# Casts of q and k placed behind a mask, and the end of the first group reordered, in a fused sliding-window attention and MLP kernel

## The chip, the cores and the metric

The kernel runs on one core of one Trainium2 chip. The metric is the device time of one execution in microseconds (us), as a median over runs. Five engines work side by side and each takes its instructions in order: TensorE (PE: matrix products and transposes), VectorE (DVE), ScalarE (ACT), GpSimd (POOL) and SyncE (SP, which here issues nearly all DMAs). An instruction that waits for another engine holds up everything behind it on its own engine.

## The reference, cut to what matters

Eight batches of attention with eight heads of 64 columns over 576 rows, each row seeing itself and the 63 rows before it; then, on the 512 columns of all heads together, a row normalisation, two matrix products with a ReLU between them, and the attention output added.

```python
scores = scale * np.matmul(q, k.transpose(0, 1, 3, 2))          # scale = 1/8
mask = (rel >= 0) & (rel < 64)                                  # rel = row - column
attn = np.exp(np.where(mask, scores, -1e9) - max)               # divided by its row sum
x = np.matmul(attn, v)                                          # heads side by side: (8, 576, 512)
xn = (x - mean(x)) / np.sqrt(var(x) + 1e-6) * g_ln
out = x + np.maximum(xn @ w_ch1, 0.0) @ w_ch2                   # 512 -> 2048 -> 512
```

Inputs and output are float32; the products run in float16 with float32 sums.

## The kernel before, in words

**Groups.** The first 512 rows of each batch are a group (0 to 7); the last 64 rows of all batches are gathered into group 8, called the tails, whose steps are numbered by pairs of batches. While the MLP of group g runs on PE, the attention of batch b = g + 1 is worked into it, and q, k and v of batch g + 2 are loaded, cast and transposed. The MLP is a list of units (`mlp_units`): for group 0 half units and row units (`l1_half`, `l1_rows`), then full units (`l1`), then the second product (`l2_three`, `l2`); for group 1 sixteen half units (first the columns of rows 0 to 255, `half` 0, then `half` 1), then `l2`; from group 2 on sixteen `l1` units and fourteen `stage` units, which make the second product in seven smaller ones from sums (`s_sums`, `w2_sums`, both on DVE).

**The order is written out by hand.** `at(i, f, ...)` puts an attention step into slot i, and slot i is issued after unit i. Within a slot the order of the `at` calls counts, engine by engine. So a step's place in the list decides both when PE comes to it and what stands behind it on every engine that it uses.

**One attention step** (a block of 128 rows, j or kb = 0 to 3) consists of
- `s_pe` (L308): 32 small score products on PE into two PSUM banks; `home` says which: `sc` (pool `ps_s`), `xps` (pool `ps_x`, two banks in one tile) or `t` (the two transpose banks t0 and t1);
- `s_exp` (L344): two exponentials on ACT into `pt`, one for each parity of the heads;
- `s_mask` (L353): one DVE product of `pt` (128x1024) with the 0/1 mask, both operands in SBUF;
- `b_pe` (L366): 16 value products on PE, again into `xps`, `sc` or `t`;
- `b_rows` (L388): on DVE the reciprocal of the row sums, the division, mean and variance; for batches 0 and 1 also z (L428), which for steps (1, 0) and (1, 1) is made on ACT (L433) in `z_step`;
- `z_step` (L421): from batch 2 on, four POOL instructions (L437 to L443);
- `zt_step` (L452): z transposed into zT, the operand of the MLP's first product. For batches 0 and 1 PE transposes into a t bank and ACT copies it out (L465); later ones are DMA transposes issued by SP.

**q and k.** `load_qk` (L84) issues the loads on SP in two halves, `cast_qk` (L141) casts each to float16 on POOL (L147, 128x1024), and `t_main` (L261) transposes: eight PE transposes into a t bank and one copy out, by ACT for q (x = 0) and DVE for k (x = 1) unless `eng` says otherwise. From batch 3 on q goes through SP's DMA transpose instead, and k is copied out by ACT. The t banks t0 and t1 alternate; from a certain unit of a group on, only t0 is used (`tbank["shared"]`), because t1 then holds a result of the second product. `add_out` (L523, L526) reads that result on DVE.

**Around the change.** At the end of group 0 slots 22 to 30 hold batch 1's value steps 0 and 1, the z rows that follow, the transposes of the second half of q and k, and the scores and exponentials of steps 2 and 3. Group 1's slot 0 holds the four casts for batch 2; its slots 2 to 7 hold value steps 2 and 3, their z rows and batch 2's transposes. In groups 2 to 5 slot 5 holds three casts for batch g + 2 (the fourth is in slot 11), and the last mask before the value steps of slot 7: step 3 of batch b in groups 2 and 4, a step of the tails in groups 3 and 5 (`TAILS`).

Of the kernel before, what the change touches and what calls it, by code (L numbers as in the profile page):

```python
# [11 lines left out]
FP16 = mybir.dt.float16  # L12
# [8 lines left out]
def kernel(  # L21
# [42 lines left out]
    mbias = p_const.tile([128, 64], FP16, tag="mbias", name="mbias")  # L64
    magt = p_const.tile([128, 4], FP32, tag="magt", name="magt")
    gT = p_const.tile([128, NKC], FP32, tag="gT", name="gT")
    mhalf = p_const.tile([128, 1], FP32, tag="mhalf", name="mhalf")
    w1g = p_const.tile([128, NKC, HID], FP16, tag="w1g", name="w1g")
    w2s = p_const.tile([128, NHC, DM], FP16, tag="w2s", name="w2s")
# [4 lines left out]
    def t_tile(shape, name):  # L74
        i = 0 if tbank["shared"] else tbank["n"] % 2
        tbank["n"] = i + 1
        return ps_t.tile(shape, FP16, tag=f"t{i}", name=name)
# [183 lines left out]
    def t_main(b, x, half, eng=None):  # L261
        src = qk16.pop((b, x, half))
        if b >= XQ and x == 0:
            dst = flat(b)[:, 2 * SM * half:2 * SM * half + 2 * SM]
            nc.sync.dma_start_transpose(out=dst.rearrange("p (a t) -> p a t", t=128),
                                        in_=src[:, :].rearrange("p a e d -> p (a e d)"))
            return
        j = 2 if b < 2 else 4
        tp = t_tile([128, 8, 128], f"tp_{b}_{x}_{half}")
        for i in range(8):  # L270
            nc.tensor.transpose(out=tp[:, i, :], in_=src[:, i], identity=ident16)  # L271
        if b < 2:
            c0 = 64 * x + 256 * half
            dst = qkT[b][x][:, :, c0:c0 + 256]
        else:
            dst = qkT[b][x][:, 2 * half:2 * half + 2, 64 * x:64 * x + 512]
        evac(x if eng is None else eng, dst.rearrange("c h (p j) -> c h p j", j=j),
             tp[:, :].rearrange("c (h j) p -> c h p j", j=j))

    def t_tail(i, x):  # L280
        src = tail16[i][x]
# [62 lines left out]
    def s_exp(g, j, *pars):  # L344
        pt, sc = pts[(g, j)], scs[(g, j)]
        for par in pars:
            o, i = pt[:, par], sc[par][:, :, :, :]
            if XQ <= g < NGRP - 1:
                o = o.rearrange("p h w (r j) -> p (h w) r j", j=4)
                i = i.rearrange("p h w (j r) -> p (h w) r j", j=4)  # L350
            nc.scalar.activation(out=o, in_=i, func=AF.Exp, bias=0.0, scale=scale)  # L351

    def s_mask(g, j):  # L353
        pt = pts[(g, j)]
# [622 lines left out]
    for g in range(NGRP):  # L977
# [7 lines left out]
        def at(i, f, *a):  # L985
            slots[min(i, len(slots) - 1)].append((f, a))
# [10 lines left out]
        if g == 0:  # L997
            at(1, zt_step, 0, 2, "dve")
            at(2, zt_step, 0, 3, "dve")
            at(4, newton, 0, 0, 4)  # L1000
            at(11, t_main, 1, 0, 0, 1)
            at(12, t_main, 1, 1, 0, 1)
            at(16, s_pe, 1, 0)
            at(16, s_pe, 1, 1, False, "xps")
            at(16, s_exp, 1, 0, 0, 1)
            at(16, s_mask, 1, 0)
            at(17, s_exp, 1, 1, 0, 1)
            at(17, s_mask, 1, 1)
            for c in range(2):
                at(20, vB_cur, 1, c, 0)  # L1010
                at(20, vB_prev, 1, c, 0)
            at(22, b_pe, 1, 0)
            at(22, b_pe, 1, 1, "sc")
            at(22, b_rows, 1, 0)
            at(22, z_step, 1, 0)
            at(23, b_rows, 1, 1)
            at(23, minus_mean, 1, 1)
            at(24, zt_step, 1, 0)
            at(25, z_step, 1, 1)
            at(26, t_main, 1, 0, 1, 0)  # L1020
            at(26, zt_step, 1, 1)
            at(27, t_main, 1, 1, 1, 1)
            at(27, vB_cur, 1, 2, 0)
            at(28, vB_prev, 1, 2, 0)
            at(28, vB_cur, 1, 3, 0)
            at(29, s_pe, 1, 2)
            at(29, s_pe, 1, 3, False, "t")
            at(29, s_exp, 1, 2, 0, 1)
            at(29, s_mask, 1, 2)
            at(30, s_exp, 1, 3, 0, 1)  # L1030
            at(30, s_mask, 1, 3)
        if g == 1:
            at(0, cast_qk, 2, 0)
            at(0, cast_qk, 2, 1)
            at(2, b_pe, 1, 2)
            at(2, b_pe, 1, 3, "sc")
            at(2, b_rows, 1, 2)
            at(3, b_rows, 1, 3)
            at(4, zt_step, 1, 2)
            at(4, root, 1)  # L1040
            at(6, zt_step, 1, 3)
            at(4, alloc_v, 2)
            at(4, alloc_qkT, 2)
            for c in (0, 2):
                at(5, cast_v, 2, c, c + 2)
                at(5, part_vB, 2, c)
            at(4, t_main, 2, 0, 0)
            at(5, t_main, 2, 1, 0)
            at(7, t_main, 2, 0, 1)
            at(7, t_main, 2, 1, 1)  # L1050
            at(7, w2_sums, 3, 0, 4)
            at(8, w2_sums, 3, 4, 8)
            at(25, w2_sums, 2, 0, 4)
            at(28, w2_sums, 2, 4, 8)
            at(9, s_pe, 2, 0)
            at(9, s_pe, 2, 1, False, "xps")
            at(9, s_exp, 2, 0, 0, 1)
            at(10, s_mask, 2, 0)
            at(11, s_exp, 2, 1, 0)
            at(12, s_exp, 2, 1, 1)  # L1060
            at(13, s_mask, 2, 1)
            for j in range(4):
                i = (14, 17, 20, 22)[j]
                if j < 3:
                    at(i, b_pe, 2, j)
                if j < 2:
                    at(i, s_mm, 2, j + 2)
                    at(i + 1, s_mask, 2, j + 2)
                if j == 2:
                    at(i, b_pe, 2, 3, "sc")  # L1070
                at(i, b_rows, 2, j)
                at(i, z_step, 2, j)
                at((18, 21, 24, 26)[j], z_act, 2, j)
                at((18, 21, 24, 26)[j], zt_step, 2, j)
            at(3, load_qk, 3, 0)
            at(8, load_qk, 3, 1)
            at(10, load_v, 3, 0, 4)
            at(8, alloc_qkT, 3)
            at(8, cast_qk, 3, 0)
            at(14, cast_qk, 3, 1, (0,))  # L1080
            at(17, cast_qk, 3, 1, (1,))
            at(22, alloc_v, 3)
            at(22, cast_v, 3, 0, 2)
            at(22, cast_v, 3, 2, 4)
            at(27, part_vB, 3, 0, 4)
            first_scores(3, 30)
            for i, (x, half) in zip((12, 24, 18, 28), ((0, 0), (1, 0), (0, 1), (1, 1))):
                at(i, t_main, 3, x, half, 0)
            at(40, load_qk, 4, 0)
            at(40, load_qk, 4, 1)  # L1090
            at(40, load_v, 4, 0, 2)
        if g == 2:
            for m, i in enumerate((1, 4)):
                at(4 + 2 * m, w2_sums, i, 0, 4)
                at(5 + 2 * m, w2_sums, i, 4, 8)
        if g > 1 and g + 2 < B:
            at(5, alloc_qkT, g + 2)
            at(5, cast_qk, g + 2, 0)
            at(5, cast_qk, g + 2, 1, (0,))
            at(11, cast_qk, g + 2, 1, (1,))  # L1100
        if g > 1 and b < B:
            tail = TAILS.get(g)
            at(2, b_pe, b, 0)
            at(2, b_rows, b, 0)
            at(2, z_step, b, 0)
            at(2, s_pe, b, 2)
            at(2, s_exp, b, 2, 0, 1)
            at(3, s_mask, b, 2)
            if tail:
                r, i = NGRP - 1, tail[0]  # L1110
                at(2, s_pe, r, i, False, "t")
                at(4, s_exp, r, i, 0)
                at(5, s_exp, r, i, 1)
                at(5, s_mask, r, i)
                at(7, b_pe, b, 1)
                at(7, b_pe, r, i, "t")
                at(7, s_mm, b, 3)
                at(7, b_rows, b, 1)
                at(7, z_step, b, 1)
                at(8, s_mask, b, 3)  # L1120
                at(8, b_rows, r, i)
                at(9, z_step, r, i)
                at(12, b_pe, b, 2)
                at(12, b_pe, b, 3, "sc")
                at(16, zt_step, r, i)
            else:
                at(2, s_pe, b, 3, False, "t")
                at(4, s_exp, b, 3, 0)
                at(5, s_exp, b, 3, 1)
                at(5, s_mask, b, 3)  # L1130
                at(7, b_pe, b, 1)
                at(7, b_pe, b, 2, "t")
                at(7, b_pe, b, 3, "sc")
                at(7, b_rows, b, 1)
                at(7, z_step, b, 1)
            at(12, b_rows, b, 2)
            at(12, z_step, b, 2)
            at(19, b_rows, b, 3)
            at(19, z_step, b, 3)
            for j in range(4):  # L1140
                at((2, 14, 18, {3: 25, 5: 25}.get(b, 23))[j], zt_step, b, j)
# [83 lines left out]
```

## Time and profile before

| what | value |
|---|---|
| median of 3 runs | 306.69 us (306.48 to 306.84) |
| the profiled execution | 306.86 us, its span 305.1 us |
| TensorE clock granted in it | 0.995 |
| casts of q and k (L147) on POOL | 30, 34.3 us busy, mean 1151 ns |
| masks (L358) on DVE | 32, 26.4 us busy, mean 831 ns |
| copies out of transposes (L257) on ACT | 17, 16.3 us busy, mean 961 ns |
| DMA queue q1 | 57.47 MB, 77.1% of 16 engines' span |

The span runs from the first to the last recorded instruction; the rest of an execution's time lies around it. A row of the timeline has the start in us from the beginning of the span, the duration in us, engine, line, operation, output and inputs with their shapes, and the number of instructions. A bracket at its end is the time that the engine stood idle just before the row, and what ended the wait. Products on PE are pipelined: the next one can start before the end that is shown for the one in front. Group 0's units begin near 21 us, group 1's near 56, group 2's near 92, and each later group takes some 31 us.

### The profile page before, as it was taken

The page shows a single profiled execution, that of the slowest core. Times are in us where ns is not written, and L with a number is a line of the kernel's source. Part 1 is how long each engine was busy: PE and PEld are TensorE (multiplying, and loading weights), DVE is VectorE, ACT ScalarE, POOL GpSimd, SP SyncE. Part 2 cuts the span into 40 slices and gives each one's busy share as a digit, 9 for nine tenths or more (in the row PEclk, how much of TensorE's full clock was granted, in tenths as well). Part 3 has the DMA queues.
Part 4 walks back from the last instruction along what each step waited for, and adds up shares of the span by engine and source line. Part 5 has one row for each costly group of instructions (what it writes and reads, how often), then busy time and mean ns, then how long its engine had stood idle before and what let it go on. Part 6 is the DMA issues. An engine that isn't in the chain of part 4 may idle for free.

```text
span 305.1 us, 7615 instructions
## 1 busy us (share of the span) xinstructions
PE 292.3 (96%) x3084; PEld 195.4 (64%) x3084; DVE 216.6 (71%) x420; ACT 155.2 (51%) x261; POOL 158.4 (52%) x230
## 2 busy tenths in 40 slices
PE   8999998999999999999999999999999999999992
PEld 3657544688454478546864686459745854788881
DVE  2879437675846896579667865697568775789972
ACT  4555655689348633874176528752575056306400
POOL 4689775451641896179509860886038407114300
PEclk9999999999999999999999999999999999999997
DMA  8999999999787898999189997992619395003014
GB/s 187 262 371 338 389 276 299 225 302 242 144 206 221 212 202 149 281 273 175 35 266 296 190 159 211 323 172 52 216 38 181 70 199 172 19 17 140 2 37 103
DMA packets 114533, 58.35 MB, mean 191 GB/s; under 512 B 83649, under 2 KB 105729, under 8 KB 114498
## 3 DMA queue, kind: packets, MB, share of 16 engines
q1 hardware_dynamic: 114208, 57.47, 77.1%
q8 instruction: 24, 0.39, 0.6%
q10 hardware_dynamic: 290, 0.40, 0.5%
q14 instruction: 11, 0.09, 0.1%
HBM read 38.80 MB, written 9.44 MB: 158 GB/s over the span
## 4 chain that ended last, share of the span: by engine, by line
PE 84%; DVE 4%; SPq 3%; ACT 3%; DMA 2%; POOL 1%; issue 1%; POOLq 0%
PE hps L504 28%; PE pA L581 12%; PE pB L581 8%; PE pC L581 8%; PE ch L516 5%; PE hph L646 5%; PE sc L341 3%; PE xps L385 3%; PE ch L681 3%; PE tp L271 2%; PE lA L719 2%; DMA w1s<-in_moe_w_ch_dram 2%; SPq L169 2%; ACT pt L351 2%; DVE pt L358 1%; SPq L89 1%
## 5 line engine op out<-in xcount | busy, mean ns | idle before, releaser
L504 PE MATMUL hps<-zT,w1g 128*128 128x512 f16 x416 | 94.7, 379 | 0.0
L508 ACT ACTIVATE hrT<-hps 128x512 f16<-128x512 f32 x104 | 62.4, 600 | 41.6 <-PE hps L504 38.3
L504 PEld LDWEIGHTS <-w1g 128*128 128x128 f16 x416 | 39.2, 98 | 45.4 <-issue 2.2
L351 ACT ACTIVATE pt<-sc 128x512 f16<-128x512 f32 x72 | 39.3, 600 | 23.2 <-PE sc L341 22.5
L437 POOL TENSOR_SCALAR rsz<-mvg 128x1 f32<-128x1 f32 x28 | 10.9, 390 | 75.1 <-DVE mvg L410 67.6
L581 PEld LDWEIGHTS <-sS 128*128 128x128 f16 x448 | 43.3, 98 | 4.9
L358 DVE TENSOR_TENSOR pt<-pt,mask 128x1024 f16<-128x1024 f16 x32 | 26.4, 831 | 21.0 <-ACT pt L351 21.0
L147 POOL CAST qk<-qk 128x1024 f16<-128x1024 f32 x30 | 34.3, 1151 | 9.2 <-DMA qk<-in_k_dram 3.3
L581 PEld LDWEIGHTS <-hrT 128*128 128x128 f16 x336 | 32.1, 98 | 6.4 <-ACT hrT L508 1.0
L257 ACT COPY qkT<-tp 128x1024 f16<-128x1024 f16 (+1 forms) x17 | 16.3, 961 | 23.8 <-PE tp L271 22.8
L581 PE MATMUL pC<-w2s,sS 128*128 128x256 f16 x224 | 26.9, 273 | 0.0
L581 PE MATMUL pA<-wT,sS 128*128 128x256 f16 x224 | 26.9, 273 | 0.0
L405 DVE TENSOR_TENSOR xn<-xps,rcp 128x256 f32<-128x256 f32 (+1 forms) x49 | 25.7, 547 | 0.8
L407 DVE BATCH_NORM_STATS2 stats<-xn 128x6 f32<-128x512 f32 x36 | 25.0, 695 | 1.2
L555 DVE TENSOR_TENSOR sS<-hrT 128x512 f16<-128x512 f16 (+1 forms) x40 | 23.7, 593 | 2.9 <-ACT hrT L508 2.9
L646 PE MATMUL hph<-zT,w1g 128*128 128x256 f16 x176 | 21.5, 273 | 0.9 <-ACT hrT L651 0.6
L401 DVE RECIPROCAL rcp<-xps 128x4 f32<-128x4 f32 (+1 forms) x49 | 7.8, 181 | 18.6 <-PE xps L385 18.6
L438 POOL TENSOR_TENSOR rsz<-rsz,mhalf 128x1 f32<-128x1 f32 x28 | 19.7, 702 | 2.3
L443 POOL TENSOR_SCALAR z<-xn,rsz 128x512 f16<-128x512 f32 x24 | 18.4, 767 | 2.5
L385 PEld LDWEIGHTS <-pt 128*64 128x64 f16 x576 | 11.6, 110 | 11.9 <-issue 5.8
L516 PE MATMUL ch<-w2s,hrT 128*128 128x512 f16 x80 | 18.8, 379 | 0.0
L646 PEld LDWEIGHTS <-w1g 128*128 128x128 f16 x176 | 16.4, 98 | 3.6 <-issue 1.1
(129 smaller groups left out, 438.2 us busy)
## 6 DMA issues: line engine op xcount, KB each, us to landing
out_dram<-xn SPq DMA_DIRECT2D x33, 256.0 KB, 3.3
qk<-in_q_dram SPq DMA_DIRECT2D x16, 512.0 KB, 6.1
qk<-in_k_dram SPq DMA_DIRECT2D x16, 512.0 KB, 6.8
v<-in_v_dram SPq DMA_DIRECT2D x28, 256.0 KB, 6.2
w2s<-in_moe_w_ch_dram SPq DMA_DIRECT2D x9, 512.0 KB, 7.8
w1s<-in_moe_w_ch_dram SPq DMA_DIRECT2D x4, 512.0 KB, 7.5
tk<-in_k_dram SPq DMA_DIRECT2D x8, 256.0 KB, 4.6
tv<-in_v_dram SPq DMA_DIRECT2D x8, 256.0 KB, 5.2
```

What stands on the lines that cost most here:

```text
L147: nc.gpsimd.tensor_copy(out=dst[:, :].rearrange("p (a j) e d -> p a e j d", j=j), in_=t[:, :].rearrange("p (a e j d) -> p a e j d", e=2, j ...
L351: nc.scalar.activation(out=o, in_=i, func=AF.Exp, bias=0.0, scale=scale)
L358: nc.vector.tensor_tensor(out=ptv, in0=ptv, in1=mb, op=ALU.mult)
L385: nc.tensor.matmul(out=tiles[h // n][64 * r:64 * r + 64, h % n, :D + 1], lhsT=pt[:, par, hp, r, :], rhs=rhs, start=True, stop=True)
L405: nc.vector.tensor_tensor(out=xn[:, n * i:n * i + n], in0=xps[:, :, 0:D], in1=rcp_b, op=ALU.mult)
L407: nc.vector.bn_stats(out=stats, in_=xv)
L504: nc.tensor.matmul(out=hps, lhsT=w1g[:, kc, 128 * hc:128 * (hc + 1)], rhs=zT[g][:, kc, :], start=(kc == 0), stop=(kc == NKC - 1),)
L508: nc.scalar.activation(out=hrT[:, hc, :], in_=hps, func=AF.Relu, bias=0.0, scale=1.0)
L516: nc.tensor.matmul(out=ch[kb], lhsT=hrT[:, hc, 128 * kb:128 * (kb + 1)], rhs=w2s[:, hc, :], start=(hc == 0), stop=(hc == NHC - 1),)
L555: nc.vector.tensor_tensor(out=o, in0=x, in1=y, op=op)
L581: nc.tensor.matmul(out=o, lhsT=a[:, c, 128 * p:128 * p + 128], rhs=wv[:, c, :], start=(first and (p == 0 or split_c) and c == 0), stop=(c ...
L646: nc.tensor.matmul(out=hps[:, e], lhsT=w1g[:, kc, 128 * hc:128 * (hc + 1)], rhs=zT[g][:, kc, 256 * half:256 * half + 256], start=(kc == 0) ...
```

## The change

The diff has two parts. In the first, a helper `after_mask` copies one element per partition of a masked `pt` tile on POOL into a new tile `masked` that nobody reads; POOL cannot run it before the mask is done. It is put ahead of the casts in slot 5 of groups 2 to 5, where it names the last mask of that slot (the calls move to a later place in the source, but stay in slots 5 and 11), and in group 1's slot 0 ahead of the last of the four casts, where it names the mask of batch 1's step 3.

In the second, for batch 1's second half, q and k are transposed into one tile in the `xps` pool (q in one bank, k in the other) instead of the t banks, and steps near them change slots. Group 0: q's transposes from slot 26 to 24, step 0's row transposes from 24 to 25, z of step 1 from 25 to 26, k's transposes from 27 to 26, step 1's row transposes from 26 to 27. The exponentials and the mask of step 3 go from the end of group 0 to slot 0 of group 1, so on ACT they stand behind the first unit's ReLU and not in front of it. Group 1: row transposes of steps 2 and 3 from slots 4 and 6 to 5 and 7, batch 2's second q transposes from 7 to 6. On PE, in the order of instructions, batch 2's q transposes now come before the rows' transposes of the same pair, and the k transposes after them.

No instruction is taken away; the five copies are all that is added.

```diff
+    masked = p_const.tile([128, 1], FP16, tag="masked", name="masked")
...
-        tp = t_tile([128, 8, 128], f"tp_{b}_{x}_{half}")
+        if (b, half) == (1, 1):
+            if x == 0:
+                both_tp[b] = ps_x.tile([128, 2, 8, 128], FP16, tag="xps", name=f"tp_{b}_{half}")
+            tp = both_tp[b][:, x]
+        else:
+            tp = t_tile([128, 8, 128], f"tp_{b}_{x}_{half}")
...
+    def after_mask(g, j):
+        nc.gpsimd.tensor_copy(out=masked, in_=pts[(g, j)][:, 1, NHP - 1, 1, 0:1])
...
-            at(24, zt_step, 1, 0)
-            at(25, z_step, 1, 1)
-            at(26, t_main, 1, 0, 1, 0)
-            at(26, zt_step, 1, 1)
-            at(27, t_main, 1, 1, 1, 1)
+            at(24, t_main, 1, 0, 1, 0)
+            at(25, zt_step, 1, 0)
+            at(26, z_step, 1, 1)
+            at(26, t_main, 1, 1, 1, 1)
+            at(27, zt_step, 1, 1)
...
-            at(30, s_exp, 1, 3, 0, 1)
-            at(30, s_mask, 1, 3)
         if g == 1:
+            at(0, s_exp, 1, 3, 0, 1)
+            at(0, s_mask, 1, 3)
             at(0, cast_qk, 2, 0)
-            at(0, cast_qk, 2, 1)
+            at(0, cast_qk, 2, 1, (0,))
+            at(0, after_mask, 1, 3)
+            at(0, cast_qk, 2, 1, (1,))
...
-            at(4, zt_step, 1, 2)
+            at(5, zt_step, 1, 2)
...
-            at(6, zt_step, 1, 3)
+            at(7, zt_step, 1, 3)
...
-            at(7, t_main, 2, 0, 1)
+            at(6, t_main, 2, 0, 1)
...
-        if g > 1 and g + 2 < B:
-            at(5, alloc_qkT, g + 2)
-            at(5, cast_qk, g + 2, 0)
-            at(5, cast_qk, g + 2, 1, (0,))
-            at(11, cast_qk, g + 2, 1, (1,))
...
+            if g + 2 < B:
+                at(5, alloc_qkT, g + 2)
+                at(5, after_mask, *((NGRP - 1, tail[0]) if tail else (b, 3)))
+                at(5, cast_qk, g + 2, 0)
+                at(5, cast_qk, g + 2, 1, (0,))
+                at(11, cast_qk, g + 2, 1, (1,))
```

More of the change, by code (lines that the diff above doesn't have):

```diff
@@ L277, in t_main @@
         evac(x if eng is None else eng, dst.rearrange("c h (p j) -> c h p j", j=j),
-             tp[:, :].rearrange("c (h j) p -> c h p j", j=j))
+             (tp if (b, half) == (1, 1) else tp[:, :]).rearrange("c (h j) p -> c h p j", j=j))
+    both_tp = {}
     def t_tail(i, x):
```

## The prediction

> **What bounds the kernel now.** I read the page's share table first, then TensorE's (PE's) own rows with the idle time in front of each, then VectorE (DVE) and GpSimd (POOL) at the same times.
>
> ```profile
> PE 292.3 (96%) x3084; PEld 195.4 (64%) x3084; DVE 216.6 (71%) x420; ACT 155.2 (51%) x261; POOL 158.4 (52%) x230
> ...
> PE 84%; DVE 4%; SPq 3%; ACT 3%; DMA 2%; POOL 1%; issue 1%; POOLq 0%
> ```
>
> PE is the bound. A reordering pays only where PE stands still, and the bracketed idle notes say where that is. The seven rows below hold 3.95 us of it at the places that the change touches.
>
> ```profile
> 48.44 0.40 PE L462 MATMUL ztp<-ident,z 128*128 128x128 f16 x4 [0.40 <-ACT z L433]
> ...
> 51.67 0.38 PE L462 MATMUL ztp<-ident,z 128*128 128x128 f16 x4 [1.09 <-DVE xn L526]
> ...
> 58.07 1.03 PE L646 MATMUL hph<-zT,w1g 128*128 128x256 f16 x8 [0.55 <-ACT hrT L651]
> ...
> 61.98 0.40 PE L462 MATMUL ztp<-ident,z 128*128 128x128 f16 x4 [0.39 <-DVE z L428]
> ...
> 132.59 0.45 PE L385 MATMUL xps<-vt,pt 128*64 128x65 f16 x16 [0.68 <-DVE pt L358]
> ...
> 164.04 0.22 PE L385 MATMUL xps<-vB,pt 128*64 128x65 f16 x1 [0.27 <-DVE pt L358]
> ...
> 195.34 0.45 PE L385 MATMUL xps<-vt,pt 128*64 128x65 f16 x16 [0.57 <-DVE pt L358]
> ```
>
> The last three are PE waiting for a mask (L358). Beside each mask stands a POOL cast of q or k:
>
> ```profile
> 130.95 1.04 POOL L147 CAST qk<-qk 128x1024 f16<-128x1024 f32 x1
> 130.97 1.56 DVE L358 TENSOR_TENSOR pt<-pt,mask 128x1024 f16<-128x1024 f16 x1 [1.97 <-ACT pt L351]
> ...
> 162.40 3.47 POOL L147 CAST qk<-qk 128x1024 f16<-128x1024 f32 x3
> 162.58 1.40 DVE L358 TENSOR_TENSOR pt<-pt,mask 128x1024 f16<-128x1024 f16 x1 [2.05 <-ACT pt L351]
> ...
> 193.70 3.61 POOL L147 CAST qk<-qk 128x1024 f16<-128x1024 f32 x3
> 193.84 1.45 DVE L358 TENSOR_TENSOR pt<-pt,mask 128x1024 f16<-128x1024 f16 x1 [2.01 <-ACT pt L351]
> ...
> 225.33 0.69 DVE L358 TENSOR_TENSOR pt<-pt,mask 128x1024 f16<-128x1024 f16 x1 [2.04 <-ACT pt L351]
> ```
>
> The fourth mask, in group 6, where no cast is queued, takes 0.69. The other three end 0.54, 0.54 and 0.55 us after the first cast's end (start + 1.04): the mask waits for the cast, whole, and then runs.
>
> **Part 1, casts behind the mask (groups 2 to 5).** Added: one POOL copy of one element per partition that waits for the mask; behind it, in POOL's order, stand three casts and then the row work of the next block. The mask starts at the same place and takes 0.66 to 0.69 instead of 1.40 to 1.56.
> Group 3: mask 130.97 to 131.63. The 16 value matmuls before it start at 131.46 and need 0.32 (the chain has 0.64 for 32 of them), so PE asks at 131.78 and need not wait: 132.59 - 131.78 = 0.81. Group 4: 163.06 + 0.64 = 163.70 against 164.04: 0.34. Group 5: 194.32 + 0.32 = 194.64 against 195.34: 0.70. Group 2: its mask (100.18, 0.75) has no PE wait behind it: 0. Sum 1.85. The bracketed idle alone gives 1.52, the lower bound; the upper is the excess of the three masks over 0.66, 0.90 + 0.74 + 0.79 = 2.43, reached only if PE waited through all of it, which the rows exclude. I take 1.85.
> What is late instead: the casts. The one-element copy isn't in this trace; POOL's nearest rows (L437, 128x1) take 0.19 to 0.54, and I take 0.3 plus 0.1 for its wait, and keep 0 to 0.6. In group 4 the first cast then starts near 163.64, not 162.40; but 0.35 of the old 3.47 was standing behind the mask (3 x 1.04 = 3.12), so the last ends 0.9 later. Group 5: 0.7 in the same way; group 2: 0.9 less what its two w2 sums (L862, 2.96 us for two) no longer lose. In group 3 the second cast starts at 132.92, after a pause that a load explains (its K load is issued at 125.24, and the page has 6.8 to landing); the first now ends by 133.1, so lateness is 0.2. Counted against a PE that is itself early by 0.3 to 0.8, the lateness is up to 1.5. It is covered by POOL's idle before later rows: 1.05 at 105.76 and 0.63 at 115.41 in group 2, 3.12 at 178.18 in group 4, 1.53 at 210.57 in group 5. If that cover is gone, the next to be late are z, its DMA transposes on SP, and behind these in SP's order the vB copies: in group 2 these are issued at 120.58 and 121.17, land 3.2 to 3.5 later, and PE uses them at 125.98, so about 1.4 more is free.
> The late casts also fall on DVE's sums (L555), which read two SBUF tensors as the mask does. In group 4 the first is at 165.69; at worst it waits one cast, 1.04. The products that need the last of these sums start at 177.57, the sum itself ends at 175.33: 2.2 of cover. Cost nothing.
> The Trainium skill, SBUF — State Buffer, section "Who interferes with whom", says that DVE with two SBUF inputs and GpSimd reading SBUF exclude each other for the whole instruction, and that whoever issues first wins. The three rows above agree (0.54 to 0.55 after the cast's end). It also speaks against the change: the little copy reads SBUF too, and a cast that is moved locks out whichever two-input DVE instruction it meets next; by that rule alone one such sum per group would be 1.04 late, and the total differs only if 2.2 us of cover were gone.
>
> **Part 2, the opening (end of group 0, start of group 1).** No instruction is removed; transposes, row copies and exponentials change places. I walk PE through it with durations of this stretch: 8 transposes 0.445, 4 z transposes 0.225, 4 products of 512 columns 0.865, two batches of scores 0.57, one half unit 0.865.
> Before, PE stood from 47.89 to 48.44 for z. Now q's transposes go there, into the value steps' bank (free since DVE's L405 ended at 46.50; the q cast ended at 47.08): 48.33. Then two products 48.77, z 48.99, four products 49.86. The k transposes follow (cast ends 49.38; they share a tile with q, so ACT's copy of q, about 48.5 to 49.5, comes first): 50.30; four products 51.17. Then PE waits for the same DVE result (L526 ends 51.62; DVE runs without a pause from 45.56 to there) and starts at the same 51.67. By then it has done the k transposes and four products more: 0.445 + 0.865 = 1.31 gained.
> From there: scores at 53.63. ACT's three casts of v end at 54.60 as before, then come the first exponentials and, moved ahead of the last ones, unit 0's ReLU, to 56.2; unit 2 starts there, not at 58.07 (1.8 gained). But the mask of step 3 is ready at 57.2, and the cast of batch 2's second q starts at 56.75, after 2.0 idle: its program waits are its load, issued at 48.56, and transposes that ended long before, so the load sets it, and it does not come earlier. It holds the mask to 57.79, and 57.79 + 0.55 = 58.34. The k cast behind it is the one that now queues. Value step 3 starts at 58.40 instead of 59.33: 0.93 is left.
> The z wait at 61.98 goes (0.57 with the hidden start): z is ready near 60.7, PE asks at 61.76. New waits come: both pairs of q and k transposes of batch 2 now follow each other in one bank, and k waits for ACT's copy of q: 0.61 + 0.06 + 1.01 + 0.06 = 1.74 from q's start, against 1.535 of PE work between: 0.2, twice. Then the second half's first unit needs the rows' copy behind that q copy and a ReLU on ACT: 0.67 + 0.90 + 0.50 + 0.59 + 0.06 = 2.72 against 1.98 + 0.2: 0.54. Together 0.94. So 0.93 + 0.57 - 0.94 = 0.56; walked row by row, batch 2's first scores start at 67.95, not 68.69 (DVE's copy held them a little before): 0.74. I take 0.65. Bounds: if the q load lands 0.6 later, 0.05; if the cast misses the mask, 1.3. Nothing from 69 to 131 makes PE wait today over 0.12, so this gain is carried on.
>
> **Sum.** 1.85 + 0.65 = 2.5. The profiled execution has 306.86 us, its span 305.1 (1.8 lies outside and stays): span near 302.6, time 304.36. The median of the runs is 306.69, 0.17 lower, so I say 304.2.
>
> **Rivals.**
> A fuller gain: the q cast misses the mask at 57.2. For it: only 0.4 us decide. Against: the 2.0 idle before 56.75. Opening 1.3: 306.69 - 3.15 = 303.5.
> Half a gain: the opening gives nothing (a later load, or ACT's queue 0.6 slower than walked) and the masks give their bracketed idle alone: 306.69 - 1.5 = 305.2. For it: four new waits in 10 us. Against: their rows are all measured.
> It doesn't do what it says: another POOL read (the z rows, L443, end 0.04 to 0.12 before these masks start) takes the casts' place and holds the mask up to 0.7: only the opening is left, 306.0. Against: both follow the same PE row by fixed distances, and group 6 has the same L443 and a free mask.
> Slower: POOL's order. The casts wait for the mask, and then each loses its turn to a DVE sum (0.68 each, four of them), so POOL is 1.3 + 4 x 0.68 = 4.0 late. It decides beyond 1.05 + 0.63 + 1.4 = 3.1 in group 2: PE then waits for vB at the next group's first value step, 0.9 there, and by like sums in the other three: 3.6 less the 2.5 gained, 307.8. For it: POOL is in order, and casts stretched to 4.38 for three at 100.34. Against: 3.12 idle at 178.18, and four lost turns in a row have no row here.
>
> **How the numbers follow.** Forecast 0.55, fuller gain 0.12, half 0.15, not as it says 0.07, slower 0.11. Forecast and both gains hold 0.82: from 302.9 (fuller, with the masks' upper end near) to 305.8 (half, with an opening that loses 0.6). About 0.2%, 0.6 us, is what can be told from no change: faster 0.82, same 0.07 (306.0 is at that edge), slower 0.11.
>
> **What would show it.** Masks in groups 3 to 5 near 0.69, and no idle over 0.15 before the value steps behind them; the casts starting 0.3 to 0.5 after the mask's end; a z transpose still held by L526 near 51.67; the mask of batch 1's step 3 ending near 58.3; a new wait of about 0.5 for ACT before the first unit of the second half of group 1. Wrong would be: a mask still over 1 us in groups 3 to 5, idle before a group's first value step or first unit, or casts of group 4 ending after 168.

## The result and the profile after

The changed kernel takes 304.37 us (median of 5 runs, 304.04 to 305.28) against 306.69 us (5 runs): a ratio of 0.9934, 95% interval 0.9912 to 0.9955. A second set of the same kernel gave 304.30 us and 0.9943 (0.9923 to 0.9963). The forecast was 304.2 us, faster; the profiled execution has 304.37 us and a span of 302.6 us, 2.5 us less than before, and 2.5 was the sum forecast. The total hides errors that cancel: the opening gave 0.3 and group 4 0.1 more than forecast, group 5 0.3 less. That the sum came out so near is partly luck.

Three lines of the page of the kernel after: the engines' busy time, the chain's shares, and the masks' group (busy us, mean ns of one, idle before).

```profile
PE 292.8 (97%) x3084; PEld 195.7 (65%) x3084; DVE 218.4 (72%) x420; ACT 154.7 (51%) x261; POOL 158.6 (52%) x235
...
PE 83%; SPq 4%; ACT 4%; DMA 3%; DVE 3%; POOL 2%; issue 1%; DVEq 0%
...
L369 DVE TENSOR_TENSOR pt<-pt,mask 128x1024 f16<-128x1024 f16 x32 | 23.9, 751 | 20.2 <-ACT pt L359 20.2
```

PE's busy time is almost the same (292.3 before). What went is idle time. The masks' mean fell from 831 to 751 ns. Line numbers have moved: the mask L358 is now L369, the cast L147 L148, POOL's z row L443 L454, the division L405 L416, DVE's sums L555 L566, the add out of the second product L594 L605; L362 is the small read.

The timeline of the kernel after, PE only, where it showed idle time before:

```profile
51.72 0.38 PE L473 MATMUL ztp<-ident,z 128*128 128x128 f16 x4 [0.35 <-DVE xn L537]
...
58.00 0.22 PE L396 MATMUL xps<-vB,pt 128*64 128x65 f16 x1 [0.29 <-DVE pt L369]
...
65.94 1.91 PE L657 MATMUL hph<-zT,w1g 128*128 128x256 f16 x16 [0.37 <-ACT zT L476]
...
192.81 0.45 PE L396 MATMUL xps<-vt,pt 128*64 128x65 f16 x16 [0.20 <-DVE pt L369]
```

Of the seven rows shown before, the waits at 48.44, 58.07, 61.98, 132.59 and 164.04 are gone. The one for L526 (now L537) shrank from 1.09 to 0.35, the one of group 5 from 0.57 to 0.20. The wait for value step 3 (58.00) and the one for ACT's copy (65.94) take the place of longer ones.

Masks, casts and small reads of the kernel after, DVE and POOL together:

```profile
55.51 1.04 POOL L148 CAST qk<-qk 128x1024 f16<-128x1024 f32 x1 [1.82 <-PE hph L657]
55.78 1.30 DVE L369 TENSOR_TENSOR pt<-pt,mask 128x1024 f16<-128x1024 f16 x1 [1.17 <-ACT pt L359]
57.25 0.69 DVE L369 TENSOR_TENSOR pt<-pt,mask 128x1024 f16<-128x1024 f16 x1 [0.17 <-ACT pt L359]
58.01 0.19 POOL L362 COPY masked<-pt 128x1 f16<-128x1 f16 x1 [1.46 <-DVE pt L369]
...
130.14 0.69 DVE L369 TENSOR_TENSOR pt<-pt,mask 128x1024 f16<-128x1024 f16 x1 [2.05 <-ACT pt L359]
130.90 0.19 POOL L362 COPY masked<-pt 128x1 f16<-128x1 f16 x1 [0.88 <-DVE pt L369]
131.02 3.46 POOL L148 CAST qk<-qk 128x1024 f16<-128x1024 f32 x3
...
157.06 0.69 DVE L416 TENSOR_TENSOR xn<-xps,rcp 128x512 f32<-128x512 f32 x1 [0.47 <-DMA out_dram<-xn]
...
160.42 0.77 POOL L454 TENSOR_SCALAR z<-xn,rsz 128x512 f16<-128x512 f32 x1
160.88 0.85 DVE L369 TENSOR_TENSOR pt<-pt,mask 128x1024 f16<-128x1024 f16 x1 [1.61 <-ACT pt L359]
...
188.08 0.69 DVE L416 TENSOR_TENSOR xn<-xps,rcp 128x512 f32<-128x512 f32 x1 [0.69 <-DMA out_dram<-xn]
191.45 0.77 POOL L454 TENSOR_SCALAR z<-xn,rsz 128x512 f16<-128x512 f32 x1
191.75 1.01 DVE L369 TENSOR_TENSOR pt<-pt,mask 128x1024 f16<-128x1024 f16 x1 [1.45 <-ACT pt L359]
```

No cast stands any more on the mask that a read names in groups 3 to 5: each waits for that mask. Group 3's mask takes 0.69 as forecast. In groups 4 and 5 another POOL instruction has moved onto the mask, the z row L454, and in both the reason stands above it: the division L416 waited 0.47 us (at 157.06) and 0.69 us (at 188.08) for an output store whose row buffer it reuses, and the whole row chain behind it came late. In the kernel before, neither division shows a wait.

**Where the time came from.** PE's lead over the trace of before can be read at the same instruction in both. I take the first `pB<-w2s` product of groups 2, 3, 4 and 5 (at 112.52, 145.02, 175.38 and 207.76 before), less the offset of the traces at the first `ch` product (36.53 before). The steps between are what each stretch gave, in us:

| kernel | median us | ratio (95%) | profiled us | opening | group 3 | group 4 | group 5 |
|---|---|---|---|---|---|---|---|
| changed | 304.37 | 0.9934 (0.9912 to 0.9955) | 304.37 | 0.96 | 0.80 | 0.45 | 0.37 |
| changed, again | 304.30 | 0.9943 (0.9923 to 0.9963) | 304.30 | 0.95 | 0.80 | 0.45 | 0.25 |
| casts only | 305.49 | 0.9958 (0.9945 to 0.9972) | 305.35 | 0.00 | 0.80 | 0.23 | 0.68 |
| opening only | 305.82 | 0.9968 (0.9952 to 0.9984) | 305.47 | 0.95 | 0.09 | 0.01 | 0.04 |
| group 1's old order | 304.25 | 0.9916 (0.9902 to 0.9930) | 303.49 | 1.71 | 0.80 | 0.46 | 0.20 |
| the same, again | 303.92 | 0.9912 (0.9896 to 0.9929) | 304.91 | 1.71 | 0.80 | 0.46 | -1.11 |
| no reads in groups 1, 2 | 304.37 | 0.9926 (0.9914 to 0.9938) | 304.65 | 0.96 | 0.87 | 0.46 | 0.16 |
| old order, no reads in 1, 2 | 304.86 | 0.9937 (0.9923 to 0.9951) | 303.53 | 1.71 | 0.87 | 0.45 | 0.25 |
| rows behind the mask too | 307.85 | 1.0038 (1.0026 to 1.0051) | 307.85 | -0.19 | 0.80 | -0.64 | -0.03 |
| order of row tiles | 304.39 | 0.9930 (0.9918 to 0.9942) | 304.38 | 0.96 | 0.80 | 0.45 | 0.40 |
| spare row buffer | 304.23 | 0.9934 (0.9912 to 0.9957) | 304.10 | 0.80 | 0.80 | 0.46 | 0.68 |
| spare buffer, old order | 303.46 | 0.9897 (0.9884 to 0.9910) | 303.49 | 1.71 | 0.80 | 0.35 | 0.33 |

For the changed kernel 0.96 + 0.80 + 0.45 + 0.37 = 2.58, less the offset of 0.05: the 2.5 of the spans. "Opening" holds all up to this product of group 2, so also what group 2's own casts cost.

### The profile page after: what moved, and what is told of

It reads as the page before. It is cut to its first block, busy times and chain, and to the rows that moved or that the text cites. A ratio compares the mean times of both kernels' runs of the same rounds, so it can differ in the third digit from the quotient of the medians.

```text
span 302.6 us, 7622 instructions
## 1 busy us (share of the span) xinstructions
PE 292.8 (97%) x3084; PEld 195.7 (65%) x3084; DVE 218.4 (72%) x420; ACT 154.7 (51%) x261; POOL 158.6 (52%) x235
## 4 chain that ended last, share of the span: by engine, by line
PE 83%; SPq 4%; ACT 4%; DMA 3%; DVE 3%; POOL 2%; issue 1%; DVEq 0%
PE hps L515 30%; PE pA L592 12%; PE pB L592 8%; PE pC L592 8%; PE ch L527 5%; PE hph L657 4%; PE xps L396 3%; PE sc L349 3%; PE ch L692 3%; DMA w1s<-in_moe_w_ch_dram 3%; PE lA L730 2%; PE tp L277 2%; SPq L170 2%; POOL w1g L224 1%; SPq L90 1%; PE lC L730 1%
## 5 line engine op out<-in xcount | busy, mean ns | idle before, releaser
L448 POOL TENSOR_SCALAR rsz<-mvg 128x1 f32<-128x1 f32 x28 | 9.7, 347 | 71.2 <-DVE mvg L421 69.2
L369 DVE TENSOR_TENSOR pt<-pt,mask 128x1024 f16<-128x1024 f16 x32 | 23.9, 751 | 20.2 <-ACT pt L359 20.2
L148 POOL CAST qk<-qk 128x1024 f16<-128x1024 f32 x30 | 33.0, 1114 | 8.6 <-DMA qk<-in_k_dram 3.5
L416 DVE TENSOR_TENSOR xn<-xps,rcp 128x256 f32<-128x256 f32 (+1 forms) x49 | 25.7, 547 | 1.9 <-DMA out_dram<-xn 1.2
L566 DVE TENSOR_TENSOR sS<-hrT 128x512 f16<-128x512 f16 (+1 forms) x40 | 24.9, 623 | 1.8 <-ACT hrT L519 1.8
L454 POOL TENSOR_SCALAR z<-xn,rsz 128x512 f16<-128x512 f32 x24 | 21.4, 893 | 2.5
L449 POOL TENSOR_TENSOR rsz<-rsz,mhalf 128x1 f32<-128x1 f32 x28 | 18.5, 661 | 2.3
L176 POOL CAST vA<-v 128x1024 f16<-128x1024 f32 (+1 forms) x18 | 15.8, 897 | 4.8 <-DMA v<-in_v_dram 4.6
```

Source lines behind the costliest of these rows:

```text
L148: nc.gpsimd.tensor_copy(out=dst[:, :].rearrange("p (a j) e d -> p a e j d", j=j), in_=t[:, :].rearrange("p (a e j d) -> p a e j d", e=2, j ...
L369: nc.vector.tensor_tensor(out=ptv, in0=ptv, in1=mb, op=ALU.mult)
L416: nc.vector.tensor_tensor(out=xn[:, n * i:n * i + n], in0=xps[:, :, 0:D], in1=rcp_b, op=ALU.mult)
L454: nc.gpsimd.tensor_scalar(out=z, in0=xv, scalar1=rs, scalar2=nm, op0=ALU.mult, op1=ALU.add)
L566: nc.vector.tensor_tensor(out=o, in0=x, in1=y, op=op)
```

## The experiments

**Casts only**: the kernel before with the reads ahead of the casts of groups 2 to 5.

```diff
+    def after_mask(g, j):
+        nc.gpsimd.tensor_copy(out=masked, in_=pts[(g, j)][:, 1, NHP - 1, 1, 0:1])
...
+                at(5, after_mask, *((NGRP - 1, tail[0]) if tail else (b, 3)))
```

> The kernel before with only the queue behind the mask in groups 2 to 5; the opening and group 1's casts as before. My theory: the three masks of groups 3 to 5 run free, and the opening has no part in it: 0.8 in group 3, 0.4 in group 4, and 0.7 in group 5, since PE does not come early enough to meet the output store of group 4 there (in the changed kernel it did, and group 5 gave only 0.37). Sum 1.9, median near 304.8. Rival (the parts lean on each other: most of the gain needs the opening): less than 1.2, above 305.5. Rival (the store is met whatever the opening does): group 5 gives 0.4 again, sum 1.6, 305.1.

It measured 305.49 us, 1.23 less than before in the same set (306.72). The theory's 304.8 missed; this is next to the rival's bound (less than 1.2, above 305.5). The trace shows a lead of 1.71 all the same, less 0.16 that was lost ahead of the first `ch` product; some 0.3 us between it and the median stays open. Its trace in group 5, where the changed kernel lost:

```profile
188.72 0.69 DVE L409 TENSOR_TENSOR xn<-xps,rcp 128x512 f32<-128x512 f32 x1
...
192.09 0.76 POOL L447 TENSOR_SCALAR z<-xn,rsz 128x512 f16<-128x512 f32 x1
193.05 0.69 DVE L362 TENSOR_TENSOR pt<-pt,mask 128x1024 f16<-128x1024 f16 x1 [2.11 <-ACT pt L352]
193.81 0.19 POOL L355 COPY masked<-pt 128x1 f16<-128x1 f16 x1 [0.96 <-DVE pt L362]
```

The division (here L409) waits for no store, the z row ends 0.20 before the mask starts, and the mask takes 0.69. With nothing in the way group 5 is worth 0.68 (forecast 0.70). Group 4 shows 0.23 of 0.45. The lead falls by some 0.23 between the last `pC` products, which begin at 152.49, and the first product of the next group, at 154.48. That product reads zT, and the DMA transpose of its z, issued at 150.05, takes 4.3 us to land, so it lands near 154.35. In the changed kernel this transpose takes 3.9 us from 149.04, and PE comes to its product at 153.17, after the landing. By these times a transfer holds the lead here too; PE's rows themselves show no wait over 0.07.

**Opening only**: the changed kernel without any read.

```diff
-            at(0, after_mask, 1, 3)
...
-                at(5, after_mask, *((NGRP - 1, tail[0]) if tail else (b, 3)))
```

> The changed kernel without any of the five small reads; all moves of the opening kept. My theory: masks of groups 3 to 5 take 1.4 to 1.6 again, and PE stands 0.3 to 0.7 behind them; the opening alone gives 0.9 less what batch 2's last k cast, no longer queued, takes from the mask of batch 1's step 3 (up to 0.6). Median 305.7 to 306.4. Rival (moving the cast calls to a later place in slot 5 is what frees the masks): near 304.4. Rival (the opening gives nothing without the read): 306.7.

It measured 305.82 us, within the forecast (305.7 to 306.4). The opening gives the same 0.95, and the masks are as long as before, with PE waiting again:

```profile
129.72 1.47 DVE L369 TENSOR_TENSOR pt<-pt,mask 128x1024 f16<-128x1024 f16 x1 [1.97 <-ACT pt L359]
...
131.24 0.45 PE L396 MATMUL xps<-vt,pt 128*64 128x65 f16 x16 [0.59 <-DVE pt L369]
```

The cast calls stand at their later place in the source here too, so it is the read that frees the masks and not that place. Both parts work alone, and the medians nearly add: 1.2 and 0.9 us, against 2.3 together.

**Group 1's old order**: the changed kernel with the row transposes and batch 2's second q transposes back in their slots.

```diff
-            at(5, zt_step, 1, 2)
+            at(4, zt_step, 1, 2)
...
-            at(7, zt_step, 1, 3)
+            at(6, zt_step, 1, 3)
...
-            at(6, t_main, 2, 0, 1)
+            at(7, t_main, 2, 0, 1)
```

> The changed kernel with group 1's rows and batch 2's second q transposes back in their old slots (4, 6 and 7). My theory: the new waits of ACT's copies in group 1 (0.2 and 0.2 for two k transposes, 0.53 for the first unit of the second half) come from this reordering alone; with the old order z of step 2 is up to 0.2 late at slot 4, the others are ready: gain 0.5 to 0.75 over the changed kernel, PE at batch 2's first scores near 67.1 instead of 67.8, median 303.6 to 303.9. Rival (the reordering is what removed the z wait of 0.39): no gain or a loss, 304.4 to 304.9.

It measured 304.25 us, with a profiled execution of 303.49. The median missed the theory's 303.6 to 303.9. The opening gives 1.71 in the trace, 0.75 more, and PE shows no wait over 0.12 between 58 and 90: the moves of group 1 brought the wait for ACT's copy at 65.94 and the smaller ones before it, and were not needed for z. In this set only 0.1 of the 0.75 came through in the median. Group 5 gave back part of it:

```profile
201.72 1.22 POOL L148 CAST qk<-qk 128x1024 f16<-128x1024 f32 x1
201.97 1.25 DVE L566 TENSOR_TENSOR sS<-hrT 128x512 f16<-128x512 f16 x1
...
203.60 0.68 DVE L605 TENSOR_TENSOR xn<-pB,xn 128x512 f32<-128x512 f32 x1
204.34 1.91 PE L592 MATMUL pB<-w2s,hrT 128*128 128x256 f16 x16 [0.27 <-DVE xn L605]
```

A cast of slot 11 stands on a DVE sum (1.25), the add that frees PE's bank comes after it, and PE waits 0.27. In this trace the division of group 5 had waited 1.21 for the store.

**Rows behind the mask too**: in groups 2 to 5 the z row of step 0 (L454), with the three POOL instructions ahead of it and the transposes of its z, also goes behind the read, so that no POOL row can stand on the mask.

```diff
-            at(2, z_step, b, 0)
+            if g + 2 >= B:
+                at(2, z_step, b, 0)
...
                 at(5, after_mask, *((NGRP - 1, tail[0]) if tail else (b, 3)))
+                at(5, z_step, b, 0)
...
-                at((2, 14, 18, {3: 25, 5: 25}.get(b, 23))[j], zt_step, b, j)
+                at((5 if g + 2 < B else 2, 14, 18, {3: 25, 5: 25}.get(b, 23))[j], zt_step, b, j)
```

> The changed kernel with the row step 0 of groups 2 to 5 (four POOL instructions and the DMA transposes of its z) moved from slot 2 to slot 5, between the small read and the casts. My theory: what still lengthens the masks of groups 4 and 5 (0.85 and 1.01) is the z row on POOL, which the late DVE row in front of it brings on top of the mask; behind the mask it cannot: masks 0.69, PE's wait of 0.20 in group 5 (0.35 with the hidden start) gone, median near 304.0, and the casts 2.5 later than in the changed kernel without cost. Rival (PE waits there for something else): 304.4. Rival (POOL's lateness is out of cover at 2.5): over 305, with PE idle before a group's first value step or first unit.

It measured 307.85 us, slower than before (1.0038, 1.0026 to 1.0051), where the theory had 304.0 and the last rival over 305. Its trace in group 2:

```profile
102.85 4.37 POOL L148 CAST qk<-qk 128x1024 f16<-128x1024 f32 x3
103.47 1.41 DVE L566 TENSOR_TENSOR sS<-sS,hrT 128x1024 f16<-128x1024 f16 x1
104.80 1.52 DVE L566 TENSOR_TENSOR sS<-hrT 128x1024 f16<-128x1024 f16 x1
106.25 1.52 DVE L566 TENSOR_TENSOR sS<-hrT,sS 128x1024 f16<-128x1024 f16 x1
...
112.57 1.69 PE L592 MATMUL pB<-w2s,hrT 128*128 128x256 f16 x14 [0.98 <-DVE xn L605]
```

The masks are clean (0.69), but the casts come 2.2 later (102.85 against 100.61) and three of DVE's sums take 1.41 to 1.52, where in the changed kernel one of them takes 1.41 and two 0.68. PE pays at the second product, 0.98 here. So this is where POOL's lateness becomes a loss: through DVE's sums and adds. The four other waits over 0.2 that PE has from there to 240 are for L605 too (0.53, 0.25 and 0.53) and for a z row (0.53, at 181.66: the last step of batches 3 and 5 is transposed by PE and not by DMA). The vB copies, which my slower rival named, did not make PE wait.

**The changed kernel again, and no reads in groups 1 and 2.** The second leaves out two of the five reads:

```diff
-            at(0, after_mask, 1, 3)
...
-                at(5, after_mask, *((NGRP - 1, tail[0]) if tail else (b, 3)))
+                if g > 2:
+                    at(5, after_mask, *((NGRP - 1, tail[0]) if tail else (b, 3)))
```

> The changed kernel once more, so that it stands beside the next three on one chip. Expected 304.4 as before, with single runs from 304.0 to 305.3. In its profile: lead of PE over the kernel before 0.9 to 1.0 from the opening, 0.8, 0.45 and 0.3 to 0.7 from groups 3, 4 and 5, the last the smaller the longer DVE's division of block 0 waits for the output store of group 4.

> The changed kernel without the small reads in groups 1 and 2. My theory: these two hide under other work and gain nothing: group 2 has no PE wait behind its mask, and in group 1 the value step waits for ACT's exponentials (mask of step 3 free at 57.2) unless batch 2's last k cast starts in that half microsecond. Median within 0.3 of the changed kernel, the lead of PE at group 3's start the same 0.9. Rival (the read in group 1 frees the opening's gain): lead at group 2's start 0.3 to 0.6, median 304.8 to 305.0. Rival (the casts' lateness in group 2 costs): faster by 0.2 or more.

304.30 and 304.37 us: these two reads are worth nothing, as forecast for group 2. The second trace of the changed kernel shows the other way in which group 5 loses:

```profile
188.27 0.69 DVE L416 TENSOR_TENSOR xn<-xps,rcp 128x512 f32<-128x512 f32 x1 [1.05 <-DMA out_dram<-xn]
191.58 0.69 DVE L369 TENSOR_TENSOR pt<-pt,mask 128x1024 f16<-128x1024 f16 x1 [1.10 <-POOL rsz L450]
191.64 1.28 POOL L454 TENSOR_SCALAR z<-xn,rsz 128x512 f16<-128x512 f32 x1
...
194.28 1.27 DVE L369 TENSOR_TENSOR pt<-pt,mask 128x1024 f16<-128x1024 f16 x1
...
205.18 1.03 PE L592 MATMUL pB<-w2s,hrT 128*128 128x256 f16 x8 [0.26 <-DVE xn L605]
```

The store came later still (1.05), so now the mask was first and the z row waited for it (1.28 for 0.77): no wait for the mask, but 0.26 later on. A later mask of the same group, at 194.28, which no read names, now meets a cast and takes 1.27 (0.76 in the first trace); PE does not wait for it.

The length of the wait for the store sorts the seven traces in which the named mask and the casts stand as here and the division of group 5 waits. With 0.67 and 0.69 (the order of row tiles below, and the first trace) the z row lands on the mask and PE waits 0.17 and 0.20 for it. With 1.05 to 1.30 (the second trace, the old order twice, no reads in groups 1 and 2, and both edits at once) PE waits 0.26 to 0.54 for the add. Without a wait for the store (casts only, and the two spare buffers) PE waits for neither.

**Order of row tiles**: a change of the order in which batches 4 and 5 get their two row tiles, meant to change which store the division waits for.

```diff
-                for h in ((1, 0) if g // 2 == 2 else (0, 1)):
+                for h in ((0, 1)):
```

> The changed kernel with the two row buffers of batches 4 and 5 handed out in the other order, so that batch 6's first block takes the buffer that group 4 stores last, and batch 5's and 7's likewise change places. My theory: DVE's division of block 0 waits 1 to 2 us longer for that store in group 5 (and 4), its z row and the casts come later by as much, the mask or the sums behind them are hit, and groups 4 and 5 together give 0.5 or less instead of 0.82; median 304.7 to 306. Rival (the store wait has nothing to do with group 5's small gain): 304.4, group 5 gives 0.37 or more.

304.39 us, and nothing follows for the store: the division of group 5 waits 0.67 for it, at 188.12, against 0.69 at 188.08 without the edit. So the edit did not change which store is waited for, and its forecast (304.7 to 306) was not put to the test; the rival's numbers (304.4, and 0.37 or more in group 5) came, but speak for nothing here. Why the edit had no effect is not shown.

**Old order, no reads in groups 1 and 2**: both edits at once.

> The changed kernel with group 1's rows and second q transposes in their old slots, and without the reads in groups 1 and 2: the opening's moves and the reads of groups 3 to 5 alone. My theory: 1.7 from the opening, 0.8, 0.45 and 0.3 to 0.7 from the masks, less up to 0.4 in group 5 where PE now meets late DVE sums: lead 3.0 to 3.6, median 303.5 to 304.0, below the changed kernel by 0.4 to 0.9. Rival (a lead of more than about 2.5 is given back to the output stores): 304.3, no faster than the changed kernel.

It missed: 304.86 us, above the theory (303.5 to 304.0), above the rival (304.3) and 0.56 above the changed kernel of the same set, though its profiled execution took 303.53, with the opening at 1.71 again. Single times of one kernel now differ by over 1 us. A profile shows only its own execution; the last run below has one of a long execution.

**Spare row buffer**: the rows of batch 6's first two steps take a buffer of the last group's rows, which stands empty then, so that the division at 188.08 waits for no store.

```diff
-                    x_norm[(g, h)] = p_xn.tile([128, 2, DM], FP32, tag="xn" + sfx, name=f"xn_{g}_{h}", bufs=nb)
+                    spare = (g, h) == (6, 0)
+                    x_norm[(g, h)] = p_xn.tile([128, 2, DM], FP32, tag="xnr" if spare else "xn" + sfx, name=f"xn_{g}_{h}", bufs=2 if spare else nb)
```

> The changed kernel with one edit: the rows of batch 6's first two steps take the second buffer of the last group's rows, so the division at 188.08 no longer waits for the store of batch 4's second half. Theory (the store's landing is what cut group 5's gain to 0.37): the division starts near 187.4, POOL's z row is over before the mask, the mask takes 0.69 and ends near 192.1, PE's lead over the kernel before grows by 0.65 to 0.70 in group 5 instead of 0.37, the 0.26 wait for VectorE's add near 205 is gone, and the time falls by 0.3 to 0.4, to a median of 303.9 to 304.1. Rival (POOL's chain behind the moved casts is full, so the late sums make PE wait at the unit of 205 whatever the mask does): the division starts early and the mask is short, but PE waits 0.26 to 0.5 near 205 and the time stays at 304.3 to 304.5.

Its trace (the division is L417 here, the z row L455):

```profile
187.40 0.69 DVE L417 TENSOR_TENSOR xn<-xps,rcp 128x512 f32<-128x512 f32 x1
190.76 0.76 POOL L455 TENSOR_SCALAR z<-xn,rsz 128x512 f16<-128x512 f32 x1
191.72 0.69 DVE L369 TENSOR_TENSOR pt<-pt,mask 128x1024 f16<-128x1024 f16 x1 [2.11 <-ACT pt L359]
```

Every link of the theory is there: the division at 187.40, the z row over at 191.52, the mask 0.69, no wait near 205, and group 5 gives 0.68 instead of 0.37. The time does not confirm it: the profiled 304.10 and the lowest of six, 303.70, are below the changed kernel's, but the median is 304.23 (303.70 to 306.03), the same within its interval. So the cause of group 5's smaller gain is shown in the trace, and its worth in the median is not.

**Spare buffer with the old order, and the old order again.**

> The spare row buffer and, in group 1, the row transposes and batch 2's second q transposes in their old slots. Theory: the opening gives 1.7 and no 0.37 wait for ACT's copy stands at 65.6; groups 3 to 5 give 0.8, 0.45 and 0.67, so PE's lead is near 3.9 at 204 and at the end; the profiled span is near 301.2, the median 303.0 to 303.6. Rival (the more PE leads, the more the loads and stores set the pace, so a lead above some 2.5 is given back): the profiled lead stays at 3.4 or lower and the median at 304.2 to 304.9, as with the old order alone.

> The kernel with group 1's old order a second time, on the chip of the two above. If its median was 304.25 because the old order helps by 0.1 only, and its profiled 303.49 was one lucky execution, the single times lie again at 304.1 to 304.5 with few near 303.5. If the old order is worth the 0.75 that its trace shows in the opening, the median comes to 303.5 to 303.8.

The combination takes 303.46 us (303.14 to 303.68), ratio 0.9897 (0.9884 to 0.9910). It is the fastest measured, 0.9 under the changed kernel, and within the theory's 303.0 to 303.6. But its traced lead, 1.71 + 0.80 + 0.35 + 0.33 = 3.19 after the offset of 0.20, is the rival's (3.4 or lower) and not the theory's 3.9. The old order again came to 303.92, between its two expectations, and this time the profile fell on its longest execution, 304.91. There, in time order:

```profile
174.84 4.32 SPq L266 DMA_TRANSPOSE qkT<-qk  x2
181.19 0.53 PE L349 MATMUL sc<-qkT,qkT 64*128 64x64 f16 x24 [0.92 <-DMA qkT<-qk]
...
188.79 0.69 DVE L416 TENSOR_TENSOR xn<-xps,rcp 128x512 f32<-128x512 f32 x1 [1.30 <-DMA out_dram<-xn]
...
205.72 0.49 PE L592 MATMUL pB<-w2s,hrT 128*128 128x256 f16 x3 [0.54 <-DVE xn L605]
```

PE waits 0.92 for the DMA transposes of q, which SP issued at 174.84 (at 173.08 in the shorter execution of the same kernel). Then the division waits 1.30 for the store, and PE 0.54 for the add: that is the -1.11 of group 5. In the combination PE waits 0.17 for the same transposes at 180.53. So with a lead of some 3 us by group 4, SP's queue and its transfers can set the pace there: by 0.92 in this execution, 0.17 in the combination's, and not at all in the shorter one of the same kernel. That this also made the other long executions, of which there is no profile, is not shown.

## Why the prediction was right, point by point

- **The masks of groups 3 and 4** (0.81 and 0.34): 0.80 and 0.45. The mechanism is shown by the two half changes: with the reads alone the masks take 0.69, without them 1.40 to 1.47. Group 4's z row stood on its mask (0.85) and yet the group gave 0.45, against 0.46 with the spare buffer, where that mask took 0.69; why it gave 0.11 more than forecast is open.
- **Group 5** (0.70): 0.37 and 0.25 in two traces of the changed kernel, 0.68 with a spare row buffer and 0.68 with the reads alone. The term was right for the instructions that I costed, but I carried PE's lead through without asking which transfer would hold it. The rival "another POOL read takes the casts' place" was this mechanism. I argued against it that mask and row follow the same PE row by fixed distances; they don't once a store stands between them. I gave this rival 0.07, and it came in part.
- **Group 2** (0): shown by leaving its read out.
- **The small read** (0.3 + 0.1): 0.19 in groups 1 and 3 to 5 and 0.59 in group 2, in groups 3 to 5 starting 0.07 after the mask's end (130.83 to 130.90); the casts behind it begin 0.19 after the mask, not 0.3 to 0.5.
- **Late casts "cost nothing"**: true in group 4, where two sums took 1.46 and 1.01 and PE did not wait. In group 5 the cover was thinner than the 2.2 taken from group 4: with the row chain late by a store wait of 1.05 us or more, PE waits 0.26 for the add, as in the second trace. The cover named (POOL's idle, then the vB copies) was the wrong one; moving POOL later by 2.2 us showed that DVE's sums run out first.
- **The opening** (0.65, bounds 0.05 to 1.3): 0.96. The wait for L526 stayed at 51.72 (51.67). The step that was off is the q cast at 56.75, of which the prediction said that its load sets it and does not come earlier: SP issued that load at 47.43 and not at 48.56, and the cast ran at 55.51 and held the mask of step 2, not of step 3. Step 3's mask ended at 57.94, not 58.34, and value step 3 started at 58.00, not 58.40. This varies: in the spare buffer's trace masks of 0.81 and 0.85 and an opening of 0.80. The new wait for ACT came as walked (0.37 shown, with the hidden start 0.53; forecast 0.54).
- **The z wait** (0.57 gained by the moves): it went, but it goes with the old order too, so the moves only cost, 0.75 in the opening of the traces; in the medians 0.1 and 0.4 of it show (304.25 and 303.92 against 304.37 and 304.30). This the prediction missed: it weighed the waits of the part as a whole, not each move against leaving it out.
- **The slower rival** (307.8, decided by POOL being beyond 3.1 late): the change itself was far from it, but the experiment that moved the z rows reached 307.85, through DVE's sums and adds instead of vB.

Forecast signs that failed: "no idle over 0.15 before the value steps" (0.20 in group 5) and masks near 0.69 in groups 4 and 5 (0.85 and 1.01). The last is just over the 1 us that the prediction named as a sign of being wrong, by the z row and not by a cast. The mask of batch 1's step 3 ended at 57.94 and not near 58.3.

## What to carry to other kernels

A read of one element orders two engines where no data does, and costs 0.19 us; price what it delays by the instructions of other engines that cannot run beside it, here DVE's sums, and not by the idle time of its own engine. When several waits are removed in a row, the lead adds up, and each later gain has to be checked against what does not move with it: stores that free buffers, transfers behind other transfers. Test each move of a group of moves by leaving it out: three of them cost 0.75 us of the lead here.

## What the runs showed of the hardware that was not expected

The exclusion between POOL and DVE has no fixed victim. The z row L454 began 0.30 before the mask and the mask lost (1.01, ending 0.54 after the row); when the mask began 0.06 before the row, the row lost (1.28 for 0.77). The Trainium skill, SBUF — State Buffer, section "Who interferes with whom", calls the port pair that DVE shares with GpSimd an exclusive lock and says that "Issue order, not op shape, decides who blocks". In these rows the one that starts second is the one that gets longer.

A store that is issued sooner lands sooner, but here by less than PE gains. Before, and then after:

```profile
184.49 2.92 SPq L542 DMA_DIRECT2D out_dram<-xn  x4
189.34 0.21 DVE L401 RECIPROCAL rcp<-xps 128x8 f32<-128x8 f32 x1 [2.16 <-PE xps L385]
189.62 0.69 DVE L405 TENSOR_TENSOR xn<-xps,rcp 128x512 f32<-128x512 f32 x1
...
182.66 2.71 SPq L553 DMA_DIRECT2D out_dram<-xn  x4
187.18 0.21 DVE L412 RECIPROCAL rcp<-xps 128x8 f32<-128x8 f32 x1 [2.16 <-PE xps L396]
```

The second of the four stores is issued at 184.91 before and at 183.28 after, and takes 4.6 and 4.7 us to land: at 189.5 and 188.0, each time about 0.1 before the division starts (189.62 and 188.08). So the landing comes 1.5 sooner, and DVE's reciprocal in front of the division 2.16 sooner; the difference is about the wait. Before, there was next to no room: the reciprocal ended at 189.55. The time to land is not fixed either: the same store takes 3.3 us with the casts only and 2.7 with the opening only, and there the division shows no wait.

The changed kernel's single times spread more than those of the kernel before: 304.03 to 306.32 in twelve runs, where before had 306.03 to 307.23 but for one run of 308.09. The combination's four lie within 0.54, and the five with the other order of row tiles within 0.21.
